# Two score regions per group of head pairs instead of three, with one score tile in two MoE banks

## The chip, the cores and the metric

The kernel runs on one core of a Trainium2 chip. The metric is device time in microseconds (us) of one execution. Times of a kernel are medians of its executions. Engines are named as in the profile: PE is the matmul engine, PEld its weight loads, DVE the vector engine, ACT the scalar engine, POOL GpSimd.

## The reference, cut to what matters

```python
# 8 batches, 8 heads, 576 tokens, head size 64
scores = scale * np.matmul(q, k.transpose(0, 1, 3, 2))
mask = block_i >= block_j            # blocks of 64 tokens, causal by block
attn = exp(where(mask, scores, -1e9) - max) ;  attn = attn / (sum(attn) + 1e-09)
x = np.matmul(attn, v)               # -> 4608 tokens x 512
# MoE part: 512 -> 1024 -> 512
h1 = x @ w1 ;  h2 = x @ w2
return np.maximum(h1, h2) @ w_out
```

## The kernel before

PE interleaves two kinds of work. *Score work* uses 64 of the 128 rows of the array for each head: two heads run side by side in two row tiles, each writing its own PSUM bank. The transposes of q, k and of the attention output (`x_out`) are 64-row work too. *MoE work* and the attention products (`av`) use all 128 rows. The kernel therefore gathers the 64-row work into "regions" and fills the time between them with MoE work.

PSUM has eight banks. Two pairs belong to the scores (`ps_s`). The other four form one ring with tag "m": every h, y, o, transposed q, k or x takes the one of the four that is released first, in program order. A tile that needs one while all four have just been used has to wait for a reader on DVE or ACT.

```python
ps_s = ctx.enter_context(tc.tile_pool(name="ps_s", bufs=2, space=bass.MemoryType.PSUM))  # 2 x 2 banks
ps_m = ctx.enter_context(tc.tile_pool(name="ps_m", bufs=4, space=bass.MemoryType.PSUM))  # 4 x 1 bank

def h_unit(i, f):                       # h1 = x w1, h2 = x w2, g = max(h1, h2)
    h1 = ...                            # SBUF tile for the first product
    for w_sb in (w1_sb, w2_sb):
        pt = ps_m.tile([P, SPAN], FP32, name="ps_h", tag="m")
        for c in range(NDM):            # 4 matmuls of 512 columns
            nc.tensor.matmul(pt[:, :w], w_sb[:, c, f * P:(f + 1) * P], xT[:, c, t0:t0 + w], ...)
            if c == NDM - 1:
                if not ph:
                    nc.vector.tensor_copy(out=h1[:, :w], in_=pt[:, :w])
                else:
                    nc.vector.tensor_max(g[:, f, m:m + w], h1[:, :w], pt[:, :w])
            ...

def tile_0(p):
    u = ps_s.tile([P, 2, 512], FP32, name="ps_s", tag="s")
    scores(p, u, 0, 0, 0, 512)          # two heads, 512 columns
    return lambda: (exp(p, u, 512, 0), mask(p, 0))
# tile_1 and tile_2: the same with 64+448 and 320+128+corner columns

for g in range(GPB, NG):                # groups 2..15, two head pairs a and b each
    a, b = 2 * g, 2 * g + 1
    if x_due:
        x_out(x_due.pop())
    n = fill_of(g)
    region(tile_0(a), tile_1(a))                                    # first region
    ...
    for p, tiles in ((a, lambda: (tile_2(a), tile_0(b))),           # second
                     (b, lambda: (tile_1(b), tile_2(b)))):          # third
        fill(hi)
        av_with(p - LAG, lo)
        copy_out = t_pair(p)            # transposes q (pair a) or k (pair b) of the next group
        outs = tiles()
        copy_out()
        region(*outs)
        pool_work(p)                    # loads, and POOL's casts of q and k to bf16
    ...
    fill(n - 2 * (lo + hi))
```

(`...` marks cuts; the special cases of the first of these groups and the padding of the keys are among what is left out.)

The softmax here doesn't subtract the row's maximum and nothing guards it: scores larger than these inputs give would overflow.

## Time and profile before

| | before |
|---|---|
| time | 283.05 us (282.59 to 287.41, 4 runs, the highest slow) |
| profiled span | 280.4 us |
| one group in the middle (start of one `x_out` to the next) | 15.01 us |
| stretches of 64-row work in the program | 61 |
| PE idle time that the profile lays to another engine, 70 to 201 us | none |

The prediction below shows the engine rows, the chain and the edges of a region. Two more views are needed for comparison. The first is the list of PE's waits in the middle (70 to 201 us): what waited, on what, us in total, times, longest.

```profile
PE ps_y L215 <- PE ps_s L321: 1.3, 8, 0.2
PE ps_h L197 <- issue: 0.2, 1, 0.2
```

Neither is a wait for another engine.

The second is the timeline through the first region of a group: start, us, engine, line, operation, times.

```profile
126.11 0.38 PE L197 MATMUL ps_h<-xT,w_sb 128*128 128x512 bf16 x1
...
126.43 0.20 PE L451 MATMUL ps_xe<-ident,xp 64*128 64x64 bf16 x1
...
126.67 0.38 PE L321 MATMUL ps_s<-qT,kT 64*128 64x512 bf16 x1
...
126.73 0.59 PE L321 MATMUL ps_s<-qT,kT 64*128 64x512 bf16 x5
...
127.25 0.82 PE L197 MATMUL ps_h<-xT,w_sb 128*128 128x512 bf16 x3
```

The whole region takes 0.83 us (126.43 to 127.25) and nothing in it waits. Its score tiles have banks of their own, whose last readers on ACT ended 3.8 and 2.8 us earlier.

### The profile page before, as it was taken

Reading aid. Unit: us, or ns where it says so; the run is one execution under the profiler, and the core shown is the slowest. Engines: PE = TensorE matmul, PEld = TensorE weight load, DVE = VectorE, ACT = ScalarE, POOL = GpSimd, SP = SyncE. Lnnn points to the kernel's source line nnn. Section 1 sums busy time; section 2 is a strip of 40 time slices with the busy share of each in tenths; the row PEclk is TensorE's granted clock in tenths of the full one; section 3 lists DMA queues with packets and bytes.
Section 4 is the critical chain, followed back from the end, with each engine's and each line's share of the span. In section 5 each row is a group of like instructions: output and inputs, shape, how many; then the busy total and the mean of one; then the engine's idle time right before and its main releaser. Section 6 shows DMA issues by size and latency. Waiting matters only on the chain.

```text
span 280.4 us, 7767 instructions
## 1 busy us (share of the span) xinstructions
PE 269.3 (96%) x3208; PEld 151.5 (54%) x3253; DVE 185.7 (66%) x386; ACT 139.6 (50%) x194; POOL 107.7 (38%) x271
## 2 busy tenths in 40 slices
PE   7699999999999999999999999999999999999995
PEld 2356766655556455555555554646455644444543
DVE  5967879668887676767667576757655766365430
ACT  3786577667664664655647374664653000100112
POOL 2996446764654625164344625371120000000000
PEclk9999999999999999999999999999999999999999
DMA  7999999979934994479266866175301111111114
GB/s 261 263 219 220 187 244 273 250 148 189 210 42 153 154 156 78 178 82 239 49 208 77 219 75 196 52 81 50 67 5 49 49 54 40 39 75 40 73 41 150
DMA packets 55940, 36.68 MB, mean 131 GB/s; under 512 B 38752, under 2 KB 43232, under 8 KB 55904
## 3 DMA queue, kind: packets, MB, share of 16 engines
q0 software_dynamic: 41728, 7.87, 35.0%
q1 hardware_dynamic: 13760, 27.66, 28.8%
q10 hardware_dynamic: 416, 0.66, 0.7%
q8 instruction: 25, 0.41, 0.6%
q14 instruction: 11, 0.09, 0.1%
HBM read 34.60 MB, written 9.44 MB: 157 GB/s over the span
## 4 chain that ended last, share of the span: by engine, by line
PE 91%; DMA 4%; issue 2%; ACT 1%; DVE 1%; POOL 0%; ACTq 0%
PE ps_h L197 43%; PE ps_y L215 22%; PE ps_o L429 11%; PE ps_s L321 8%; DMA vv<-in_v_dram 2%; PE ps_xe L451 2%; PE ps_qT L303 2%; DMA qraw<-in_q_dram 2%; PE ps_kT L303 2%; ACT aT L345 1%; PE ps_s L339 1%; PE ps_y L231 1%; PE ps_w L292 1%; DVE g L206 0%; POOL vv L133 0%
## 5 line engine op out<-in xcount | busy, mean ns | idle before, releaser
L197 PE MATMUL ps_h<-xT,w_sb 128*128 128x512 bf16 (+3 forms) x605 | 136.2, 357 | 1.7 <-issue 0.3
L345 ACT ACTIVATE aT<-ps_s 128x1024 bf16<-128x1024 f32 (+2 forms) x100 | 96.2, 996 | 17.2 <-PE ps_s L321 16.2
L197 PEld LDWEIGHTS <-w_sb 128*128 128x128 bf16 x640 | 57.8, 98 | 57.4 <-issue 8.1
L204 DVE CAST h<-ps_h 128x512 bf16<-128x512 f32 (+3 forms) x80 | 50.9, 637 | 28.9 <-PE ps_h L197 26.7
L215 PE MATMUL ps_y<-wo_sb,g 128*128 128x512 bf16 x273 | 65.5, 379 | 2.1 <-PE ps_s L321 1.3
L206 DVE TENSOR_TENSOR g<-h,ps_h 128x512 bf16<-128x512 bf16 (+3 forms) x80 | 50.6, 632 | 12.0 <-PE ps_h L197 10.5
L350 POOL MEMSET aT<- 64x128 bf16 x124 | 22.3, 199 | 92.7 <-ACT aT L345 91.3
L221 ACT COPY y<-ps_y 128x512 f32<-128x512 f32 x31 | 18.1, 584 | 70.3 <-PE ps_y L215 56.5
L429 PEld LDWEIGHTS <-aT 128*128 128x128 bf16 x960 | 37.3, 98 | 14.1 <-issue 1.3
L215 PEld LDWEIGHTS <-g 128*128 128x128 bf16 x280 | 26.8, 98 | 30.4 <-issue 1.1
L429 PE MATMUL ps_o<-vv,aT 128*128 128x65 bf16 x960 | 39.9, 194 | 0.3 <-DMA vv<-in_v_dram 0.3
L133 POOL DMA_DIRECT2D vv<-in_v_dram x40 | 33.7, 847 | 0.5
L436 DVE TENSOR_TENSOR xp<-ps_o,rec 128x256 bf16<-128x256 f32 (+1 forms) x64 | 31.4, 491 | 2.2
L321 PE MATMUL ps_s<-qT,kT 64*128 64x64 bf16 (+6 forms) x344 | 31.6, 279 | 1.1 <-ACT kT L310 0.7
L435 DVE RECIPROCAL rec<-ps_o 128x4 f32<-128x4 f32 (+1 forms) x64 | 12.0, 188 | 20.6 <-PE ps_o L429 18.9
L310 ACT COPY qT<-ps_qT 128x576 bf16<-128x576 bf16 x15 | 9.6, 638 | 29.4 <-PE ps_qT L303 29.4
L187 POOL COPY g<-g 128x512 bf16<-128x512 bf16 x8 | 4.9, 611 | 38.3 <-DVE g L206 38.2
L129 POOL CAST kn<-kraw 128x1152 bf16<-128x1152 f32 x15 | 17.3, 1151 | 5.2 <-DMA kraw<-in_k_dram 5.1
L129 POOL CAST qn<-qraw 128x1152 bf16<-128x1152 f32 (+1 forms) x15 | 16.5, 1099 | 7.0 <-DMA qraw<-in_q_dram 6.9
L456 DVE COPY xT<-ps_xe 128x640 bf16<-128x640 bf16 (+2 forms) x18 | 8.2, 453 | 15.7 <-PE ps_xe L451 14.9
L310 ACT COPY kT<-ps_kT 128x576 bf16<-128x576 bf16 x15 | 9.6, 638 | 15.0 <-PE ps_kT L303 15.0
L321 PEld LDWEIGHTS <-kT 64*128 64x128 bf16 x344 | 13.2, 95 | 6.6 <-issue 2.8
(44 smaller groups left out, 144.5 us busy)
## 6 DMA issues: line engine op xcount, KB each, us to landing
qraw<-in_q_dram SPq DMA_DIRECT2D x16, 576.0 KB, 4.1
out_dram<-y SPq DMA_DIRECT2D x35, 256.0 KB, 2.1
kraw<-in_k_dram SPq DMA_DIRECT2D x15, 576.0 KB, 5.4
vv<-in_v_dram POOLq DMA_DIRECT2D x32, 128.0 KB, 5.3
w_sb<-in_moe_w_dram POOLq DMA_DIRECT2D x4, 256.0 KB, 6.6
w_sb<-in_moe_w_dram POOLq DMA_DIRECT2D x2, 512.0 KB, 10.7
wo_sb<-in_moe_w_out_dram POOLq DMA_DIRECT2D x2, 512.0 KB, 11.8
kraw<-in_k_dram ACTq DMA_DIRECT2D x1, 576.0 KB, 5.4
```

What stands on the lines that cost most here:

```text
L129: copy(out=n[:, j0:j1], in_=t[:, j0:j1])
L133: nc.gpsimd.dma_start(out=vv_r[b % NV][P - rows:, c, :, :D], in_=v[b, :, c * P:c * P + rows, :].rearrange("h p d -> p h d"),)
L197: nc.tensor.matmul(pt[:, :w], w_sb[:, c, f * P:(f + 1) * P], xT[:, c, t0:t0 + w], start=(c == 0), stop=(c == NDM - 1),)
L204: nc.vector.tensor_copy(out=h1[:, :w], in_=pt[:, :w])
L206: nc.vector.tensor_max(g[:, f, m:m + w], h1[:, :w], pt[:, :w])
L215: nc.tensor.matmul(py[:], g[:, f, s * P:(s + 1) * P], wo_sb[:, f, :], start=(f == 0), stop=(f == NFF - 1),)
L310: copies[i](out=t[:, :S].rearrange("q (p j) -> q p j", j=RPP), in_=pts[i].rearrange("q j p -> q p j"),)
L321: nc.tensor.matmul(ps[:, hh, col:col + w], kT[r, k0:k0 + P], qT[r, q0:q0 + w], start=True, stop=True,)
L345: nc.scalar.activation(out=aT_r[p % NA][:, :, a0:a0 + w], in_=ps[:, :, :w], func=AF.Exp, scale=scale,)
L350: (eng or nc.gpsimd).memset(aT_r[p % NA][BLK:, :, a0:a0 + BLK], 0.0)
L429: nc.tensor.matmul(po[:, gi, hh, :], a[:, hh, a0:a0 + P], vv[:, c, h0 + 2 * hh, :], start=(mm == 0), stop=(mm == n_mm - 1),)
L436: nc.vector.tensor_mul(xp[:, ts[0]:ts[0] + n, :, p % 2], po[:, :, :, :D], rec[:, :n].to_broadcast([P, n, 2, D]),)
```

## The change

The intent is to enter 64-row mode twice instead of three times a group, since PE drains at each change of mode (0.096 us a change in the trace; the prediction shows how it is read). All three tiles of a pair then have to run in one region, but the score banks hold two. So tile 0 goes into two of the four MoE banks, one for each head. To make those free as early as possible, its matmul on the bank that is used later comes first, the fill closes the accumulation that is open before the region, tile 1 and the output transposes run ahead of it, and one of the two output copies moves from DVE to ACT.

```diff
+    inside = [...]                       # is this step inside an open accumulation?
-    def fill(n):
-        while n > 0 and at[0] < len(steps) and steps[at[0]][1] <= done_tokens[0]:
+    def fill(n, whole=False):
+        while at[0] < len(steps) and steps[at[0]][1] <= done_tokens[0]:
+            if n <= 0 and not (whole and inside[at[0]]):
+                break
+    def tile_0m(p):
+        us = [ps_m.tile([P, 512], FP32, name="ps_s0", tag="m") for _ in range(2)]
+        for hh in (1, 0):
+            r = slice(hh * D, (hh + 1) * D)
+            nc.tensor.matmul(
+                us[hh][:], kT_r[p % NT][r, :P], qT_r[p % NT][r, :512], start=True, stop=True)
+
+        def out():
+            for hh in range(2):
+                nc.scalar.activation(
+                    out=aT_r[p % NA][:, hh, :512], in_=us[hh][:], func=AF.Exp, scale=scale)
+            mask(p, 0)
+        return out
-        nc.vector.tensor_copy(out=dst[:, :, :, 0], in_=pe[:])
-        nc.vector.tensor_copy(out=dst[:, :, :n_odd, 1], in_=po[:])
+        copies[0](out=dst[:, :, :, 0], in_=pe[:])
+        copies[1](out=dst[:, :, :n_odd, 1], in_=po[:])
     for g in range(GPB, NG):
-        (three regions, as above)
+        fill(0, True)
+        for p in (a, b):
+            if p == a and x_due:
+                x_out(x_due.pop(), copies=(act, dve))
+                n = fill_of(g)
+            if p == a:
+                out1 = tile_1(a); out0 = tile_0m(a); out2 = tile_2(a)
+                copy_out = t_pair(a) if g > GPB else (lambda: None)
+                out0(); out1(); copy_out(); out2()
+            else:
+                copy_out = t_pair(b)
+                out1 = tile_1(b); out0 = tile_0m(b); out2 = tile_2(b)
+                copy_out(); out1(); out0(); out2()
+                ... (pad_keys as before)
+            pool_work(p)
+            ...
+            fill(hi * 3 // 5)
+            av_with(p - LAG, lo)
+            fill(hi - hi * 3 // 5, True)
```

(Semicolons join lines that are separate in the kernel; `...` marks cuts.)

More of the change, by code (lines that the diff above doesn't have):

```diff
@@ L270 @@
     steps = [(u, need, cost) for u, need, cost, n in units for _ in range(n)]
+    inside = [j % (NDM if n > NFF or n == 2 * NDM and u.__name__ == "h_unit" else NFF) > 0
+              for u, _, _, n in units for j in range(n)]
     at = [0]
@@ L439, in av, with x_out @@
         )
-    def x_out(g, t0=0, t1=NCH):
+    def x_out(g, t0=0, t1=NCH, copies=(dve, dve)):
         b, u = divmod(g, GPB)
@@ L590 @@
         a, b = 2 * g, 2 * g + 1
-        if x_due:
-            x_out(x_due.pop())
         n = fill_of(g)
-        region(tile_0(a), tile_1(a))
-        if g == GPB:
-            av(3, [2, 3, 4])
-            fill(5)
-            x_out(1, 2, NCH)
-            n = fill_of(g)
-        lo, hi = max(3, n // 18), n * 2 // 9
-        for p, tiles in ((a, lambda: (tile_2(a), tile_0(b))), (b, lambda: (tile_1(b), tile_2(b)))):
-            fill(hi)
+        fill(0, True)
[4 more added lines that the diff above has]
+            if p == a:
+                out1 = tile_1(a)
+                out0 = tile_0m(a)
+                out2 = tile_2(a)
+                copy_out = t_pair(a) if g > GPB else (lambda: None)
+                out0()
+                out1()
+                copy_out()
+                out2()
+            else:
+                copy_out = t_pair(b)
+                out1 = tile_1(b)
+                out0 = tile_0m(b)
+                out2 = tile_2(b)
+                copy_out()
+                out1()
+                out0()
+                out2()
+                if g + 1 < NG:
+                    pad_keys(p + 1)
+                    pad_keys(p + 2)
+            pool_work(p)
+            if g == GPB and p == a:
+                av(3, [2, 3, 4])
+                fill(5)
+                x_out(1, 2, NCH)
+                t_pair(a)()
+                n = fill_of(g)
+            lo = max(3, n // 18)
+            hi = max(0, n // 2 - lo)
             if g > GPB:
+                fill(hi * 3 // 5)
                 av_with(p - LAG, lo)
+                fill(hi - hi * 3 // 5, True)
             else:
-                fill(lo)
-            copy_out = t_pair(p)
-            outs = tiles()
-            copy_out()
-            region(*outs)
-            if p % 2 and g + 1 < NG:
-                pad_keys(p + 1)
-                pad_keys(p + 2)
-            pool_work(p)
+                fill(lo + hi, True)
         if g > GPB:
             x_due.append(g - 1)
-        fill(n - 2 * (lo + hi))
     for p in range(NPAIR - LAG, NPAIR):
```

## The prediction

> **What bounds the kernel now.** I read the engine rows and the strip first, then the chain, then stretches of equal length, then the timeline round one score region.
>
> ```profile
> PE 269.3 (96%) x3208; PEld 151.5 (54%) x3253; DVE 185.7 (66%) x386; ACT 139.6 (50%) x194; POOL 107.7 (38%) x271
> ...
> PE   7699999999999999999999999999999999999995
> ...
> PE 91%; DMA 4%; issue 2%; ACT 1%; DVE 1%; POOL 0%; ACTq 0%
> ```
>
> The matmul engine is busy nearly throughout and is 91% of the chain that ended last; the other engines have a third or more to spare. Two neighbouring stretches in the middle, columns PE, PEld, DVE, ACT, POOL, clock, DMA share, GB/s:
>
> ```profile
> 155.00:170.00 15.00, 14.74 (x189) 8.28 (x190) 10.20 (x21) 8.62 (x12) 6.62 (x18) 1.00 0.70 137
> 170.00:185.00 15.00, 14.74 (x189) 8.25 (x190) 10.20 (x21) 8.62 (x12) 6.61 (x16) 1.00 0.63 134
> ```
>
> They are one group (two head pairs) each: the output transposes begin at 171.45, 186.46 and 201.47, so a group takes 15.01 us. So the middle is paced by how densely PE is fed, and a change there counts at full value. What PE loses between instructions shows at the edges of a region:
>
> ```profile
> 200.94 0.59 PE L197 MATMUL ps_h<-xT,w_sb 128*128 128x512 bf16 x2
> ...
> 201.46 0.09 PEld L451 LDWEIGHTS <-xp 64*128 64x128 bf16 x1 [0.42 <-issue]
> ...
> 201.47 0.20 PE L451 MATMUL ps_xe<-ident,xp 64*128 64x64 bf16 x1
> ...
> 196.32 0.36 PE L321 MATMUL ps_s<-qT,kT 64*128 64x320 bf16 x4
> 196.61 0.39 PE L197 MATMUL ps_h<-xT,w_sb 128*128 128x512 bf16 x1
> ```
>
> Inside a run a 512-column matmul starts 0.216 us after the one before it. The second ps_h of the pair starts at 201.16 and the 64-row transpose at 201.47: 0.312, so 0.096 more. Leaving 64-row work costs the same: in the trace a 128-column score matmul is followed by ps_h after 0.148, against 0.053 of streaming (128 columns at 512 per 0.213). One stretch of 64-row work thus costs 2 x 0.096 = 0.19 us.
>
> The last rows I need show how long a bank stays taken after its last matmul, and what a wait looks like when it binds:
>
> ```profile
> 216.28 1.03 PE L197 MATMUL ps_h<-xT,w_sb 128*128 128x512 bf16 x4
> ...
> 217.34 0.69 DVE L206 TENSOR_TENSOR g<-h,ps_h 128x512 bf16<-128x512 bf16 x1 [0.17 <-PE ps_h L197]
> ...
> 218.08 1.24 PE L197 MATMUL ps_h<-xT,w_sb 128*128 128x512 bf16 x4
> ```
>
> Call T the start of the last matmul into a bank (216.28 + 3 x 0.216 = 216.93). The maximum starts 0.41 to 0.43 after T, runs 0.69, and the next matmul that needs the bank starts 0.05 after its end (218.03 to 218.08). So the bank is usable again at T + 1.17. Before has this wait only in the tail and early; in the middle PE never stands still for a bank.
>
> **What the Trainium skill says.** "TensorEngine Tiling (Array Packing)", Key Properties: changing the tiling mode drains the engine. The trace agrees, at 0.096 us a change. Its "Gotcha 1: PSUM Pressure" says that different row tiles need different banks, which is why one more score tile in flight needs two of them; the trace shows the two halves running side by side (six score matmuls from 186.76 on, 2048 columns in all, are followed by ps_h at 187.29: 0.53 with the mode change, where 2048 columns one after another would stream for 0.85). "Perfetto Trace Analysis", Per-engine timelines: a reported end of VectorE or ScalarE leaves out the semaphore's propagation; the 0.05 us above is that. "ScalarE: Activation LUTs", What ACT_TABLE_LOAD costs: an activation with immediate operands takes a fixed 186 ns and 0.833 ns an element. The trace agrees nearly: 1.026 us for 1024 columns (1.04), 0.584 for a 512-column copy (0.61).
>
> **The change part by part.**
>
> (1) Stretches. Before has three 64-row stretches for a group, after two: each pair now runs its three tiles together, with the transposes of q or k and the output transposes joined to them. The instruction order of the built kernel confirms it: same 6508 PE rows, 14 fewer 64-row stretches. Gain: 14 x 0.19 = 2.7 us. That is the whole intended gain, 0.95%.
>
> (2) The third tile in two of the four MoE banks. A "whole" fill now closes the last MoE unit before each region. In the built order, from group 6 to 14, every section ends with two complete h groups, then the region starts. The free banks go to the two transposes; the two score halves get the banks of exactly those two h groups. The half issued first takes the w1 bank (its cast has ended); the other waits for the maximum on the w2 bank, usable at T + 1.17. What can PE do until then? Last h 0.216 + mode change 0.096 + output transposes 0.245 (201.47-type start to scores, 186.46 to 186.70) + tile 1 0.216 (64 and 448 columns, two halves at once) = T + 0.77. Stall 0.40. In the second region of a group the key transposes (0.28, 195.77 to 196.05) stand in place of the output ones: stall 0.37. The half issued first does not help: the two halves would have run at once, and everything after waits behind the second.
>
> (3) The bank after the region. In the first region the first h group after it takes the bank of the late half, free when its exponential ends. That half starts at T + 1.17, its exponential 0.43 to 0.48 later (ps_s to ACT in this trace), 512 columns take an estimated 0.60 (between 0.489 for 384 and 0.814 for 768 in this trace), 0.05 to PE: T + 2.28. PE would be there at 1.17 + 0.216 + tile 2 0.245 + query transposes 0.25 + 0.12 = T + 2.00. Stall 0.28. In the second region that place is held by a key copy, done by then: none.
>
> (4) Copies. One of the two output copies, 0.49 on DVE, goes to ACT at an estimated 0.69 (0.638 for 576 elements there); 28 exponentials of 1024 columns become 56 of 512, an estimated +0.1 each. ACT goes from 8.6 to some 9.6 us of a group, under 15: no bound of its own there, and it keeps the output bank from waiting behind the maximum on DVE.
>
> (5) Groups 2 to 5. There sections are short, some with only eight or sixteen long matmuls (1.7 to 3.5 us plus 0.9 of attention products), and end with a y unit, whose copy stands on ACT behind the exponentials of the region before (about 4.8 us). Working that queue through by the same durations gives about 2.1 us of waiting in the three regions round group 4, and three regions of groups 2 and 3 add 0.9, 5b its 0.37.
>
> Sum: first regions of groups 6 to 14, 9 x (0.40 + 0.28) = 6.1; second regions 9 x 0.37 = 3.3; group 15, whose second region gets older banks, 0.4; early groups 3.4. Waits 13.2, less 2.7 saved: +10.5 us, 283.2 to about 294. A steady group: 15.0 - 0.19 + 0.40 + 0.28 + 0.37 = 15.9 us.
>
> **Rivals.** A: the plain reading of the change; only the drains count, 280.5. For it: the author ordered tile 1 and the transposes ahead to give DVE time, and split the copies. Against: 0.77 us of work cannot cover 1.17, and nothing else sits between. B: the drains are saved and about half of the waits are real, because PE's lead over DVE is smaller than I take it or the fills end elsewhere than I think: 288 to 290. For it: the early regions are my weakest sums. Against: the steady section repeats nine times in the built order and its durations vary by a per cent. C: ACT becomes the bound in the short early groups and loses several us there, 297 or more. For it: some 10 us of ACT work against 9 to 10 of PE in group 4. Against: before has the same squeeze and shows no such wait between 36 and 218 us.
>
> **Range and chances.** 294, with 288.5 to 298 for eight in ten: the low end is B, the high end C. Slower by over 2% means above 288.9. Chances: faster 0.03, same 0.13, slower 0.84.
>
> **What would show it.** Steady groups of 15.9 us; PE's busy share in a stretch of a group down from 14.74 of 15.0 to some 95%; the score matmuls of the new tile waiting about 0.4 us for the maximum's line (or its wait shown as DVE g), 18 or more times; ps_h waiting 0.3 us for an exponential after every first region; 14 fewer drains; the tail after the last region unchanged at about 65 us. If the steady group comes out at 14.8, step 2 is wrong and A holds; if the middle is as I say but the total isn't, it is step 5.

## The result and the profile after

| | before | after |
|---|---|---|
| time | 283.05 us (282.59 to 287.41, 4 runs, the highest slow) | 293.88 us (293.35 to 295.06, 4 runs) |
| ratio | | 1.0394, 95% interval 1.0352 to 1.0436 |
| profiled span | 280.4 us | 292.0 us |
| one group in the middle | 15.01 us | 15.75 us |
| stretches of 64-row work | 61 | 47 |

The kernel became slower by 3.9%; the prediction said 294.0.

The engine rows, the strip and the chain of the changed kernel:

```profile
PE 278.2 (95%) x3210; PEld 151.6 (52%) x3253; DVE 181.9 (62%) x374; ACT 147.8 (51%) x234; POOL 107.5 (37%) x271
...
PE   8799989999999999999999999999999999999995
...
PE 84%; DMA 5%; ACT 4%; issue 2%; DVE 2%; POOL 1%; SPq 0%; ACTq 0%; DVEq 0%
```

PE fell from 91% to 84% of the chain; ACT rose from 1% to 4%. ACT is still busy only 51% of the span, so it isn't the bound: it appears in the chain because PE now waits for it at single places. The busy rows hardly show the loss. PE looks *busier* than before (278.2 against 269.3 us) with the same 3253 matmuls in the program. The reason stands in a group's stretch (columns PE, PEld, DVE, ACT, POOL, clock, DMA share, GB/s):

```profile
119.74:135.49 15.75, 15.36 (x190) 8.25 (x192) 10.00 (x19) 9.33 (x15) 6.90 (x18) 1.00 0.60 128
135.49:151.24 15.75, 15.35 (x188) 8.24 (x191) 9.86 (x19) 9.33 (x15) 6.26 (x17) 1.00 0.65 129
```

The same work as in a group of before is now called 15.36 us busy instead of 14.74. (A part of this is only missing records: split_max_before, with a group of the same length as before, shows 15.01.) The first region shows why:

```profile
134.53 1.03 PE L197 MATMUL ps_h<-xT,w_sb 128*128 128x512 bf16 x4
...
135.59 0.69 DVE L206 TENSOR_TENSOR g<-h,ps_h 128x512 bf16<-128x512 bf16 x1 [0.17 <-PE ps_h L197]
...
135.95 0.76 PE L342 MATMUL ps_s<-qT,kT 64*128 64x512 bf16 x2
...
136.34 0.23 PE L358 MATMUL ps_s<-qT,kz 64*128 64x64 bf16 x2
...
136.74 0.48 PE L307 MATMUL ps_qT<-ident,qn 64*128 64x64 bf16 x18
...
136.80 1.09 ACT L347 ACTIVATE aT<-ps_s 128x512 bf16<-128x512 f32 x2
...
137.45 0.38 PE L197 MATMUL ps_h<-xT,w_sb 128*128 128x512 bf16 x1 [0.23 <-ACT aT L347]
```

The two matmuls of L342 are tile 0, one for each head. Side by side they should begin together and take 0.38 in all (as they do early in the trace, at 40.20, where nothing holds their banks); here they take 0.76. The second begins 0.380 after the first, at 136.33, because its bank is the one that the maximum of L206 reads from 135.59 to 136.28. The first is called busy for 0.37 of that time, so PE's row has no gap. The next wait does show: the ps_h at 137.45 starts 0.422 after the last query transpose, against 0.12 where nothing waits. Its bank is that of the late half. The first of the two exponentials of L347 reads it, starts at 136.80 and takes 0.60, so it ends at 137.40.

PE's waits in the changed kernel's middle (76 to 214 us) name only the second of these, nine times in nine groups:

```profile
PE ps_h L197 <- ACT aT L347: 2.1, 9, 0.2
```

The first one is found in the waits of the weight loader, in the same window. It has no names there but the count is telling: 18 times, twice a group, in front of the instruction that follows tile 0 (L358):

```profile
PEld L358 <- issue: 7.8, 18, 0.4
```

To see where the 11.6 us between the two profiled spans came from, I counted the columns of all matmuls in program order, at the pace of the trace (a 512-column matmul every 0.216 us; 64-row work two by two). Both kernels come to the same sum, about 253 us, so the differences between the two columns are what counts here; "the end" is the start of the last matmul. The start of a stretch less the work ahead of it is what PE has lost until then:

| lost by the start of | before | after | difference | grew by |
|---|---|---|---|---|
| the last stretch that both have alike (26 us) | 10.08 | 10.52 | 0.44 | 0.44 |
| group 4 | 12.64 | 15.44 | 2.80 | 2.36 |
| group 6 | 14.38 | 19.15 | 4.77 | 1.97 |
| group 15 | 22.06 | 33.54 | 11.48 | 6.71 |
| the end | 23.80 | 35.39 | 11.59 | 0.11 |

The 0.44 is there before the first instruction differs (it lies in the first loads, and varied from -0.2 to +1.2 over the runs below). The nine groups 6 to 14 lose 0.74 each, very evenly; the four before them lose 4.3 together, and unevenly.

### The profile page after: what moved, and what is told of

The parts are those of the page before. It is cut to its first block, busy times and chain, and to the rows that moved or that the text cites. A ratio compares the mean times of both kernels' runs of the same rounds, so it can differ in the third digit from the quotient of the medians.

```text
span 292.0 us, 7823 instructions
## 1 busy us (share of the span) xinstructions
PE 278.2 (95%) x3210; PEld 151.6 (52%) x3253; DVE 181.9 (62%) x374; ACT 147.8 (51%) x234; POOL 107.5 (37%) x271
## 4 chain that ended last, share of the span: by engine, by line
PE 84%; DMA 5%; ACT 4%; issue 2%; DVE 2%; POOL 1%; SPq 0%; ACTq 0%; DVEq 0%
PE ps_h L197 42%; PE ps_y L215 20%; PE ps_o L448 10%; PE ps_s L325 4%; PE ps_s L342 4%; ACT aT L347 3%; DMA vv<-in_v_dram 3%; DMA kraw<-in_k_dram 3%; PE ps_kT L307 2%; PE ps_xe L470 2%; PE ps_y L231 1%; DVE xp L455 1%; ACT aT L364 1%; DVE g L206 0%; POOL qn L129 0%
## 5 line engine op out<-in xcount | busy, mean ns | idle before, releaser
L197 PEld LDWEIGHTS <-w_sb 128*128 128x128 bf16 x640 | 59.3, 98 | 59.7 <-issue 5.5
L364 ACT ACTIVATE aT<-ps_s 128x1024 bf16<-128x1024 f32 (+2 forms) x72 | 71.1, 998 | 7.6 <-PE ps_s L325 7.5
L215 PE MATMUL ps_y<-wo_sb,g 128*128 128x512 bf16 x265 | 69.6, 379 | 1.1 <-ACT aT L347 0.2
L206 DVE TENSOR_TENSOR g<-h,ps_h 128x512 bf16<-128x512 bf16 (+3 forms) x80 | 50.6, 633 | 12.9 <-PE ps_h L197 10.6
L215 PEld LDWEIGHTS <-g 128*128 128x128 bf16 x280 | 24.7, 98 | 23.6 <-issue 0.6
L325 PE MATMUL ps_s<-qT,kT 64*128 64x320 bf16 (+5 forms) x288 | 31.6, 261 | 1.1 <-ACT kT L314 0.7
L347 ACT ACTIVATE aT<-ps_s 128x512 bf16<-128x512 f32 x56 | 30.5, 602 | 3.7 <-PE ps_s L342 2.5
L342 PE MATMUL ps_s<-qT,kT 64*128 64x512 bf16 x56 | 19.2, 374 | 0.2
L314 DVE COPY qT<-ps_qT 128x576 bf16<-128x576 bf16 x17 | 12.9, 757 | 9.8 <-PE ps_qT L307 9.7
```

Source lines behind the costliest of these rows:

```text
L215: nc.tensor.matmul(py[:], g[:, f, s * P:(s + 1) * P], wo_sb[:, f, :], start=(f == 0), stop=(f == NFF - 1),)
L325: nc.tensor.matmul(ps[:, hh, col:col + w], kT[r, k0:k0 + P], qT[r, q0:q0 + w], start=True, stop=True,)
L342: nc.tensor.matmul(us[hh][:], kT_r[p % NT][r, :P], qT_r[p % NT][r, :512], start=True, stop=True)
L347: nc.scalar.activation(out=aT_r[p % NA][:, hh, :512], in_=us[hh][:], func=AF.Exp, scale=scale)
L364: nc.scalar.activation(out=aT_r[p % NA][:, :, a0:a0 + w], in_=ps[:, :, :w], func=AF.Exp, scale=scale,)
```

## The experiments

Each kernel was run with 3 rounds beside the kernel before; every result below is correct. Theory: PE reaches tile 0's later half before the maximum on its bank has ended, and reaches the next h before the exponential on that same bank has. Rivals: the moved copy, the split exponentials, the closing of accumulations, or ACT's queue cost the time.

**1. fill_wait: put work into the wait.** Tile 1's 448 columns are issued three times instead of once, which changes no result. That adds 0.37 us of matmuls ahead of tile 0 in each region.

```diff
         scores(p, u, 64, 1, 128, 448)
+        for _ in range(2):
+            scores(p, u, 64, 1, 128, 448)
```

> The changed kernel with tile 1's pair of 448-column score matmuls issued three times instead of once in each of the 28 regions (the repeats write the same numbers again). That is 0.37 us of extra PE streaming a region, 10.5 us in all. Theory (PE stands at the second half of the new tile for 0.38 and 0.35 us until the maximum has freed its bank): the extra work lies inside that wait, so the steady group stays at 15.75 us within 0.1, the gap between the halves falls from 0.38 and 0.35 to about nothing, and the total goes from 293.9 to 294 to 295.5 (only the regions without a wait, and a rest of 0.03 in the others, pay). Rival (the time went to something other than these gaps, PE being short of time itself): every repeat costs, about +10 us, 304.

Measured: 295.95 us (295.41 to 296.85), ratio 1.0449. A steady group:

```profile
104.60:120.44 15.84, 15.61 (x200) 8.76 (x200) 9.85 (x19) 9.34 (x15) 6.25 (x17) 1.00 0.67 133
```

The group grew by 0.09 us for 0.75 us of extra matmuls. The wait between the halves is gone: in the second regions they start 0.003 apart. In the first regions 0.055 is left, but the same 0.055 stands in before too, right after the output transposes (126.673 and 126.728 above), so it is no wait for the maximum. The gap at the exit stayed at 0.423 us. So the wait for the maximum is real and hides nearly all of this extra work. The total came out 0.5 above the range I gave, since regions without a wait pay for theirs: by the trace 0.9 of the 2.1 us came before group 6, 0.8 in the nine steady groups and 0.4 after.

**2. split_max_after: make the maximum longer.** The maximum is taken in two halves.

```diff
-                        nc.vector.tensor_max(g[:, f, m:m + w], h1[:, :w], pt[:, :w])
+                        for c0, c1 in ((0, w // 2), (w // 2, w)):
+                            nc.vector.tensor_max(
+                                g[:, f, m + c0:m + c1], h1[:, c0:c1], pt[:, c0:c1])
```

> The changed kernel with each maximum of the MoE cut into two halves of the columns, so the second h bank comes free later by about 0.16 us (2 x 0.42 in place of 0.69). Theory: each of the about 21 regions that wait for a maximum waits 0.16 longer, also those whose next wait hangs on it: the gap between the halves goes to about 0.54 and 0.51, the steady group to about 16.05, the total to about 297 (+3 to +4). Rival (the wait for the maximum is not what sets the time, DVE being only 62% busy): no change within 0.5 us.

Measured: 295.93 us (295.29 to 296.57), ratio 1.0445. The two halves of the maximum, the two halves of tile 0 behind them, and the weight load between:

```profile
121.48 0.75 DVE L207 TENSOR_TENSOR g<-h,ps_h 128x256 bf16<-128x256 bf16 x2 [0.17 <-PE ps_h L197]
...
121.84 0.84 PE L344 MATMUL ps_s<-qT,kT 64*128 64x512 bf16 x2
...
122.28 0.09 PEld L344 LDWEIGHTS <-kT 64*128 64x128 bf16 x1 [0.51 <-DVE g L207]
```

The maximum lasts 0.75 instead of 0.69, and the gap between tile 0's halves grew by just as much, from 0.380 to 0.447. The region grew by 0.08, the group by 0.16. This one edit also gave the wait its name. In the changed kernel the weight of tile 0 was loaded before the wait; here it is loaded after it, and the loader's waits read:

```profile
PEld L344 <- DVE g L207: 9.2, 18, 0.5
```

That is the maximum, 18 times, in the two regions of nine groups. My size was off by half: I had counted 0.16 for each region and got it for each group, because the second half begins before the first has ended in the records.

**3. split_max_before: the control.** The same edit in the kernel before.

> The kernel before with each maximum cut into two halves: the control for the same cut in the changed kernel. DVE gets some 13 us more work. Theory: before never waits in the middle for a bank freed by the last maximum, so its steady group stays 15.01 us and the total within 1 us of 283 (some of the few early and late waits may grow). Rival (longer DVE work costs as such): +3 us or more, as in the changed kernel.

Measured: 282.43 us (282.27 to 282.86), ratio 0.999 (0.9954 to 1.0026), a group 15.01 us. The length of the maximum matters only where tile 0 lies in the MoE banks.

**4. older_banks: give tile 0 the older banks.** The output and key transposes come after tiles 1, 0 and 2, so that tile 0 takes the two banks that have been free longest.

```diff
             if p == a:
-                (output transposes)
                 out1 = tile_1(a); out0 = tile_0m(a); out2 = tile_2(a)
+                (output transposes)
                 ...
```

> The changed kernel with the order turned: tile 1, the two halves of the new tile, tile 2, and only then the transposes. The halves then get banks freed long ago (the built program shows it), the transposes those of the last two h. Theory: the wait between the halves vanishes, but four banks still have to turn over within a region, so it moves: transposes wait 0.18 for the maximum, in first regions the query transposes wait about 0.7 for the exponentials, in second regions h waits 0.1. Net +0.2 in first and -0.07 in second regions: steady group 15.9, total 294 to 296. Rival (it is only the choice of the bank, and an older bank is enough): steady group below 15.1, total about 284 to 286.

Measured: 296.3 us (295.65 to 296.55), ratio 1.0455, a group 16.0 us; the total is 0.3 above the expected range. The first region:

```profile
120.64 0.38 PE L342 MATMUL ps_s<-qT,kT 64*128 64x512 bf16 x2
...
121.80 0.19 PE L307 MATMUL ps_qT<-ident,qn 64*128 64x64 bf16 x1
122.29 0.42 PE L307 MATMUL ps_qT<-ident,qn 64*128 64x64 bf16 x17 [0.30 <-ACT aT L347]
```

Tile 0's halves now run together, in 0.38. But the output transposes take the banks of the last two h and wait for the maximum in their place, and the query transposes take tile 0's own banks and wait for its exponentials. A first region asks for six MoE banks (two output, two tile 0, two query) out of four. By this count, in any order, the last two take banks that the region itself has just filled, and two take those of the last h pair. The order moves the wait and doesn't remove it.

**5. reorder: finish sooner.** Exponentials in the order in which the halves finish; in the second region tile 2 goes before tile 0.

```diff
         def out():
-            for hh in range(2):
+            for hh in (1, 0):
             ...
             else:
-                out1 = tile_1(b); out0 = tile_0m(b); out2 = tile_2(b)
+                out1 = tile_1(b); out2 = tile_2(b); out0 = tile_0m(b)
```

> The changed kernel with two turns: in second regions tile 2's matmuls ahead of the new tile (0.245 us of useful work inside the wait), and the exponentials of the new tile in the order in which its halves are done. Theory: the gap in second regions falls from 0.35 to about 0.1; in first regions h waits for the early half's exponential, about 0.1 instead of 0.30. Steady group 15.3, total about 289.5. It does not reach the kernel before. Rival (the wait is a fixed cost of the merged region, whatever lies in it): no change, 293 to 295.

Measured: 290.32 us (289.81 to 291.17), ratio 1.0267, a group 15.40 us. The first region's exit gap fell from 0.422 to 0.215: the next h now takes the bank of the half that was ready early, since that one's exponential comes first. In the second region the wait for the maximum is covered by tile 2:

```profile
127.74 0.36 PE L325 MATMUL ps_s<-qT,kT 64*128 64x320 bf16 x4
127.93 0.47 PE L342 MATMUL ps_s<-qT,kT 64*128 64x512 bf16 x2
128.46 0.59 PE L197 MATMUL ps_h<-xT,w_sb 128*128 128x512 bf16 x2
```

The halves take 0.47 in all instead of 0.72. A smaller wait is new here: the last h in these rows starts 0.42 after the late half where 0.31 is usual, because in the built program it shares a bank with a key copy on ACT, which ended 0.05 earlier, at 128.41. That is about 0.1 a group. This is the best form with two regions throughout. It still loses 0.39 a group against before, mostly by the first region's wait for the maximum, which is unchanged at 0.38. The list of PE's waits for this kernel's middle is empty: none of that shows there.

**6. x_dve: both output copies on DVE again.**

```diff
-                x_out(x_due.pop(), copies=(act, dve))
+                x_out(x_due.pop(), copies=(dve, dve))
```

> The changed kernel with both output copies back on DVE. Theory: they then run after the maximum, one behind the other, so the second bank for the query transposes comes free at T + 2.08 instead of T + 1.5: the transposes wait about 0.44, the wait for the exponential behind them is swallowed, net +0.15 us a first region: steady group 15.9, total 294.5 to 295.5. Rival (the move to ACT is itself a cause of the loss, since ACT's queue delays the exponentials): faster than 293.9 by 1 us or more.

Measured: 293.85 us (293.52 to 294.88), ratio 1.0368, a group 15.75 us: no change, where I had expected +0.15 a group. The query transposes do meet the second copy now (a gap of 0.27 between two of them), but the h behind them then waits that much less (0.155 instead of 0.422); it has to wait for the exponential's end either way. The move of the copy to ACT neither costs nor gains.

**7. before_act: the ACT part alone.** In the kernel before, tile 0's exponential in two halves and one output copy on ACT.

> The kernel before with the changed kernel's ACT work: the even output copy on ACT, and tile 0's exponential in two halves of 512. Theory: ACT has room, nothing on PE waits for it: steady group 15.0, total within 0.7 us of 283. Rival (the extra ACT work is a good part of the loss): +2 us or more.

Measured: 283.15 us (282.75 to 284.39), ratio 1.0018 (0.9979 to 1.0056), a group 15.01 us with ACT busy for 9.34 us of it, as in the changed kernel. ACT's extra work costs nothing by itself.

**8. before_whole: the closing alone.** In the kernel before, the new `fill`, with `fill(0, True)` ahead of each region.

> The kernel before, its three regions kept, but the MoE accumulation that is open is closed before every region, as in the changed kernel. Theory: closing alone costs little, since no score tile takes the bank that was just closed; the transposes take older ones: within 1.5 us of 283. Rival (closing, not the banks, exposes the evacuation): +5 us or more.

Measured: 285.07 us (284.29 to 285.43), ratio 1.0075, so +2.1 us, more than I had allowed. In the profile 0.9 of it is already there at 22 us, before anything differs. Another 1.0 comes between 23 and 52 us, where closing a y unit pulls its last matmuls ahead of the weights that they need:

```profile
50.70 1.02 PE L215 MATMUL ps_y<-wo_sb,g 128*128 128x512 bf16 x4 [0.71 <-DMA wo_sb<-in_moe_w_out_dram]
```

The changed kernel has no such wait for w_out. In the steady groups the closing costs about 0.09 us each. It is a minor part.

**9 and 10. late_two and early_two: which groups lose how much.** late_two runs three regions in groups 2 to 5 and two from group 6 on; early_two the other way round.

```diff
     for g in range(GPB, NG):
+        if g < 6:            # early_two: g >= 6
+            (body of before)
+        else:
             (body of the changed kernel)
```

> Three regions in groups 2 to 5, two regions from group 6 on. Theory (steady loss by the waits for a bank is 0.74 us a group, nine groups 6 to 14, and the early groups lose 4.3 for reasons of their own): 283 + 6.7 + about 0.3 = 290.0 us, between 289.3 and 290.8. Rival (the early groups only started an offset that the steady groups would also show alone, or the early arrears change what is left for the later fill): outside that interval, 292 or more, or 288 or less.

> Two regions in groups 2 to 5, three from group 6 on. Theory: 283 + 4.3 + about 0.3 = 287.5 us, between 286.8 and 288.3; the steady group is at 15.0 us again. Rival: the early loss is made up later when the region form changes (under 286).

Measured: late_two 289.84 us (289.53 to 290.55), ratio 1.0258; early_two 287.94 us (286.94 to 289.64), ratio 1.0193 (1.0153 to 1.0233: slower, but whether by 2% is unclear). One group in the middle, first of late_two, then of early_two:

```profile
99.57:115.33 15.76, 15.36 (x188) 8.26 (x190) 9.82 (x19) 9.33 (x15) 6.27 (x17) 1.00 0.66 130
```

```profile
101.73:116.74 15.01, 14.75 (x189) 8.27 (x192) 10.20 (x20) 8.62 (x13) 6.62 (x18) 1.00 0.69 136
```

The loss follows the form of the region, group by group, and is not made up later. Both totals are in the expected ranges. By ratio the two losses are 7.3 and 5.5 us of 282.65 and add up to 12.8, 1.7 more than the changed kernel's 11.1; in the profiles each of them has 0.9 us of it at 22 us, where the changed kernel has 0.44.

**11. early_cast: the early groups' own wait.** In the changed kernel two query transposes of the early groups (groups 3 and 5) wait for POOL's cast of q:

```profile
40.06 1.15 POOL L129 CAST qn<-qraw 128x1152 bf16<-128x1152 f32 x1
...
41.27 0.44 PE L307 MATMUL ps_qT<-ident,qn 64*128 64x64 bf16 x18 [0.45 <-POOL qn L129]
```

In before the same cast ran at 38.78, and its transposes, behind the fill and the attention products, at 41.41, without a wait. Here the cast is issued ahead of the last masks in groups 2 and 4.

```diff
                 out1()
                 out0()
+                if g in (2, 4):
+                    cast("q", g + 2, ((pool, 0, RPP),))
                 out2()
```

> The changed kernel with GpSimd's cast of q in groups 2 and 4 ahead of the last masks of the region, about 1.2 us sooner. Theory (the query transposes of groups 3 and 5, pulled ahead of the fill, meet this cast: waits of 0.45 and 0.35 us): both waits go, total 0.6 to 0.9 us less than the changed kernel, 293.1. Rival (they would meet DVE or ACT, or the next bank, instead): the two transposes begin as late as before and the total is within 0.2 of it.

Measured: 293.46 us (293.34 to 294.37), ratio 1.0381: within the interval of the changed kernel's 1.0394, so not told apart by time. In the trace the two places went different ways. In group 5 the cast's wait is gone and its region shrank from 2.46 to 2.23 us. In group 3 the cast was now too early: its load had not landed, the key padding queued behind it on POOL, and the region stood still for longer:

```profile
42.21 0.23 PE L358 MATMUL ps_s<-qT,kz 64*128 64x64 bf16 x4 [1.58 <-POOL kz L332]
```

So the cast is shown as a cause in group 5 (0.23 us). In group 3 the earlier cast can't be had by this order, and the time of its wait stays a reading of the trace.

No version with two regions came near 283 us.

## Why the prediction was right

By its own steps:

1. *Fourteen stretches fewer, 0.19 us each.* Right: 61 stretches became 47. By the trace a steady group's growth of 0.74 fits: of the first gap of 0.380 between halves, 0.055 stands there without any wait (experiment 1), so the three waits make 0.33 + 0.35 + 0.30 = 0.98, less 0.19 is 0.79.
2. *Tile 0's later half waits for the maximum, 0.40 and 0.37 us.* Right in mechanism and nearly in size: gaps of 0.380, of which the wait is some 0.33, and 0.350. fill_wait showed that there is idle time to fill, split_max_after that its length follows the maximum's, split_max_before that only this placement depends on it.
3. *The h behind the query transposes waits for the late half's exponential, 0.28 us.* Right: 0.30 (0.422 against 0.122), and reorder took 0.21 of it away by emptying the early half first, so that the h takes that one's bank.
4. *The copies and split exponentials are no bound.* Right: before_act changed nothing, and x_dve nothing either. Why the copy's return to DVE is free, I had not seen.
5. *Groups 2 to 5: 3.4 us of waits less 0.8 of stretches, 2.6 net.* The direction was right, the size and the named reason were not: 4.33 us. The text had about 2.1 of waiting round group 4, because a y unit's copy would stand on ACT behind the exponentials. In the trace the four y copies of groups 4 and 5 (52.6 to 63.5 us) ran on DVE, not on ACT: the kernel gives the y copies of the first two spans to DVE. The waits there are others. Three times a late half of tile 0 starts 0.05 after such a copy on DVE ended:

```profile
63.50 0.68 DVE L221 COPY y<-ps_y 128x512 f32<-128x512 f32 x1
...
64.05 0.56 PE L342 MATMUL ps_s<-qT,kT 64*128 64x512 bf16 x2
```

   The halves start 0.385, 0.355 and 0.185 apart at these places. Besides, a y waits 0.30 for an exponential, output transposes 0.28 for DVE and query transposes 0.35 for POOL's cast. Together that is 1.9, near the predicted 2.1 but by other waits, so that agreement is luck. With the 0.35 of group 5's second region, less 0.38 for two stretches, it makes 1.9 net; 1.97 was measured.

   Groups 2 and 3, with 0.9 of waits predicted, gave 2.36 net. The term of the sum that was mis-sized is those "three regions of groups 2 and 3". What it left out is that a merged region also pulls the query transposes ahead of the fill and the attention products that used to come before them. In the trace they wait 0.42 us at 31.5, for an output copy by the profile (POOL's cast ended only 0.03 earlier, so either would have held them), and 0.45 for the cast at 41.3, and the halves of the second region of group 3 start 0.49 apart at 46. These three make 1.36. Four more starts of an h (32.71, 37.70, 43.29, 48.89) come 0.05 after an ACT instruction that held their bank, a query copy or an exponential, and are late by about 1.1 us together; before has about 0.5 of such waits in these groups. No experiment tested these, and the sum of groups 2 and 3 is not closed.

The steady groups in turn were put at 15.9 and came out at 15.75: nine times 0.74 is 6.7, where the prediction's terms make 7.7. The two errors, -1.0 and +1.7, partly cancel, so the total is better than its parts.

Of the rivals, A (only the drains count) would have needed a shorter group; it grew. B (half of the waits real) is ruled out by the steady gaps. C (ACT as the bound early) is not what the early waits name: ACT is the releaser of 0.4 us among PE's listed waits between 27 and 76 us. The list leaves out the four starts above, about 1.1 us; with them it is still far from the several us, and the 297, of C.

Two readings in the prediction are not quite right, and nothing hangs on them. Its six score matmuls start at 186.70, not 186.76, so they take 0.58 us to the ps_h, not 0.53, which is still well under 0.85. And the trace gives only the 0.05 us from an end on DVE to the next start on PE; that this is the semaphore's propagation alone, no run shows.

One sign that the prediction gave was the wrong one to look for. PE's busy share fell to 97.5% (15.36 of 15.75), not to "some 95%". The wait lies under a record that is itself counted as busy, and 14.74 of 15.00 was an undercount: in split_max_before, whose trace holds more of the matmul records, a group of the same length has 15.01 us of PE in 15.01.

## What to carry to other kernels

Before taking a bank out of a ring in use, write down when its last reader ends, and how much work PE has until it gets there; here 0.77 us of work stood against 1.17, twice a group, and a saved 0.19 us could not pay for it. If a region needs more banks than its ring has, reordering only moves the wait: what helps is to put independent work between the last writer and the next user, or to empty the tiles in the order in which they are ready (reorder did both). And when several pieces of work are joined, ask of each what it used to wait behind: moving it forward may bring it to a producer on another engine that is not done.

## What the Trainium skill lacked or had wrong

- "TensorEngine Tiling (Array Packing)", Key Properties, says that a change of tiling mode drains the engine, without a size. Here it is 0.096 us each way, 0.19 for one stretch: small beside one bank wait of 0.38.
- The same page's "Gotcha 1: PSUM Pressure" says that row tiles write different banks and that software must synchronise. It lacks what that means with two banks that come free at different times: issuing the half with the free bank first gains nothing by itself (0.76 us for two halves that take 0.38), and all later work on PE waits too.
- "Perfetto Trace Analysis", Per-engine timelines, says that PE's end times are estimated. The trace agrees; what the page lacks is that with row tiles a wait between two halves vanishes from PE's busy row (15.36 of 15.75 us busy with gaps of 0.38 and 0.35 between halves) and from its list of waits. It is seen in the start-to-start time of the halves, or at the weight loader (18 times 0.4 us).
- No page that I read gives the way from the last matmul into a bank to the bank's reuse: 0.42 us from that matmul's start to the start of the DVE maximum, 0.69 for the maximum, 0.05 to PE, so 1.16 us the whole way.
